# Order of the second-layer sums, of GpSimd's joins and of the splits in a fused attention, expert and softplus kernel

## The chip, the cores and the metric

The kernel runs on one core of one Trainium2 chip. A core has TensorE (matrix products, results in the eight banks of PSUM), VectorE, ScalarE, GpSimd and SyncE, each with an instruction queue of its own that it works through in order; work on different engines is ordered by semaphores. GpSimd does not read PSUM here. The metric is the time of one execution on the device in microseconds, median of the timed runs.

## The reference

Three stages, each feeding the next. Everything is float32, the last stage's weights come as 64-bit floats.

```python
# attention: q, k, v of (4, 8, 576, 64); k and v averaged over groups of 8 positions
attn = softmax(q @ mean8(k).T / sqrt(64));  x = attn @ mean8(v)        # -> (2304, 512)
# 8 experts, all of them for every token, with shares P from 8 rounds of row and column scaling
P = balanced(exp(x @ w_gate))
out = sum(P[:, e:e+1] * (relu(x @ w1[e]) @ w2[e]) for e in range(8))   # 512 -> 1024 -> 512
# softplus stage
return softplus(out @ w_in) @ w_out                                   # 512 -> 2048 -> 512
```

## The kernel before

**Arithmetic.** Every float32 product is made of three products in a shorter format: each operand is split into a rounded part (`hi`, by ScalarE) and the remainder (`lo`, by VectorE or GpSimd), and hi*hi, lo*hi and hi*lo are added in PSUM (`three`, L794). On top of that the large products are done by Winograd's form of Strassen's scheme: a 2 x 2 block product from seven products of sums of blocks.

**Phases and units.** The 2304 tokens are three groups of 768 (`PAIRS`). There are six phases: the expert stage for the three groups (phases 0, 1, 2), then the softplus stage for them (3, 4, 5). A phase of the expert stage has 32 units, one for each 256 columns of the hidden layer (4 to an expert), a softplus phase has 8. A unit `n` has a first part (x times its columns of `w1`) and a second part (the hidden columns times `w2`). The order of the parts is `first 0, first 1, second 0, first 2, second 1, ...` (`todo`).

**Phases 1 and 2** apply the seven-product scheme in both layers, the second over a pair of units, even and odd (`first_twice`, `second_twice`). The first part of a unit is seven products of six matmuls, in the order A11, A22, S2, S1, A12, S3 and, as `rest`, S4. They stand in two double banks of PSUM: `d1` holds `pa` and `pd_`, `d2` holds `pc` and `pb`. A12 goes on top of `pa`, S3 on top of `pb`, S4 on top of `pc`. VectorE adds: `u1 = pb + a` (L865) before S3 is added onto `pb`, then `a = pb + a`, `pb = pc + a`, `pd_ = pd_ + a`, and after S4 `pc + u1`. `a` is a copy of `pa` that ScalarE makes.

**The posts.** The blocks of a finished pair are scaled by the tokens' shares (`shared`, L886) and become seven operands, q to q+6, each with `hi` and `lo`: two from the even unit's blocks and one difference (`even_posts`), the other four with the odd unit's (`odd_posts`). The last step at once is `p3` (L933): two remainders, and then the subtraction of `s3` from `d2` into `s3` (L936). The operands q+4 to q+6 are left in the list `later` as s2, s4, s1 and one more remainder, and `run_later` does them in the first part of the next even unit, right behind u1 (L866). s1 (L943) adds `d2` to `a21`; s4 (L948) subtracts `s3` from `d1`, in its bank.

**Banks.** The first parts of pairs take the double banks of kind R and L in turn (two each), and the form products of the second parts take the other kind: two of them in the even unit's second part (q, q+1), five in the odd unit's (q+2 to q+6), each 12 matmuls. A bank is handed on in the order in which its last reader was issued, so the first of the five form products takes the bank of `d1` or `d2` that was let go first. Behind the first form product of a second part comes S4 of the unit that is under way (`go_on`).

**Beside that**, three kinds of work are handed out by `between(k)`, called after the k-th product of a first part: `to_split` (in the last unit of a phase: the seven splits of the next phase's inputs, a ScalarE cast and a load of the remainder from `xlod` on SyncE's queue), `joins` (GpSimd's sums of blocks for the next phase, in even units; `load_x` and pauses are in this list too), and in odd units `hook` or `convert` (VectorE's conversion of the softplus weights from 64 bits, 32 chunks over the whole kernel, six steps each; those missing when a weight is to be loaded are done at once by `needed`). After the first part come the casts and remainders of the next `w1` (`prep_w1`) and the load of the one after it (`load_w`). In the second parts of phase 0 and of phases 3 to 5 `hook` is called behind each 128 tokens; its argument says whether it may convert.

Of the kernel before, what the change touches and what calls it, by code (L numbers as in the profile page):

```python
# [19 lines left out]
def attention_moe_softplus_kernel(  # L20
# [12 lines left out]
    nc = tc.nc  # L33
# [814 lines left out]
    def first_twice(n, between):  # L848

        product = product_of(n)  # L850
        a, u1 = (zpool.tile([P, TB], F32, tag="z", name=x) for x in ("za", "u1"))
        kind = "RL"[sets[n][3] // 2 % 2]
        d1 = two_banks(kind, "p")
        pa, pd_ = d1[:, 0], d1[:, 1]
        product(pa, A11, "b11")
        between(0)
        product(pd_, A22, "t4")
        nc.scalar.copy(a, pa)
        between(1)
        d2 = two_banks(kind, "p")  # L860
        pc, pb = d2[:, 0], d2[:, 1]
        product(pb, S2, "t2")
        between(2)
        product(pc, S1, "t1")
        vadd(u1, pb, a)  # L865
        run_later()  # L866
        between(3)
        product(pa, A12, "b21", True)
        between(4)
        product(pb, S3, "t3", True)  # L870
        vadd(a, pb, a)
        vadd(pb, pc, a)
        vadd(pd_, pd_, a)
        between(5)
        two_t[n] = d1, d2

        def s4():
            product(pc, S4, "b22", True)
            vadd(pc, pc, u1)

        return s4
# [6 lines left out]
    def form_hi(q, src):  # L888
        nc.scalar.copy(h_slot(q)[0], src)  # L889
# [27 lines left out]
    def odd_posts(n):  # L917

        f, _, _, u = sets[n]
        q = pair_of_units(n) * FORMS  # L920
        d1, d2 = two_t.pop(n)

        def p1():
            shared(d1, d1, 0)
            form_hi(q + 2, d1)

        def p2():
            shared(d2, d2, 1)
            form_hi(q + 3, d2)
            if u % UPE == UPE - 1:  # L930
                load_shares(TWICE.index(f) * E + u // UPE + 1)

        def p3():  # L933
            form_lo(q + 2, d1, nc.vector)
            form_lo(q + 3, d2, nc.vector)
            vsub(s3_t(), d2, s3_t())  # L936

        def s2():
            form_hi(q + 5, s3_t())
            form_lo(q + 5, s3_t(), nc.gpsimd)  # L940

        def s1():
            vadd(a21_t(), d2, a21_t())  # L943
            form_hi(q + 4, a21_t())
            form_lo(q + 4, a21_t(), nc.gpsimd)

        def s4():
            vsub(d1, d1, s3_t())  # L948
            form_hi(q + 6, d1)

        later.extend([s2, s4, s1, lambda: form_lo(q + 6, d1, nc.vector)])
        return [p1, p2, p3]

    def m_at(f, k):
# [601 lines left out]
    for step, (what, n) in enumerate(todo):  # L1556
# [3 lines left out]
        if what == "first":  # L1560
            nxt = sets[n + 1] if n + 1 < len(sets) else None
            if n and sets[n - 1][0] != f:
                xs.update(xs_next)
                xs_next.clear()
            if nxt is not None and n:
                sums_w1(n + 1)
            if nxt is not None and nxt[0] != f:
                flush()
                to_split = splits(x_for(nxt[0]), t_in(t_at[nxt[0]], nxt[2]), f=nxt[0])

            if twice(n):
                if not twice(n - 1):
                    while not between_chunks[0]:
                        convert()
                    settled()
                    open_banks("right", ("R", 2))
                    open_extra(
                        ("hhi", [P, 2 * TB], F32R), ("hlo", [P, 2 * TB], F32R), ("whi", [P, UC * HALF], F32R),
                        ("wlo", [P, UC * HALF], F32R), ("a21", [P, 2, TB], F32), ("s3", [P, 2, TB], F32),
                    )  # L1580

                def between(k):

                    if to_split and k in (1, 3, 4, 5):
                        to_split.pop(0)()
                    if u % 2 == 0:
                        if k == 2:
                            settled()
                        if joins and k in (1, 4):
                            joins.pop(0)()  # L1590
                        return
                    if k == 0:
                        sharing[0] = not side
                        pause[0] = 0
                    if not sharing[0]:
                        hook()
                    elif (k == 0 and u < NU1 - 1) or not between_chunks[0]:
                        convert()

                away[0] = "LR"[u // 2 % 2]  # L1600
                rest = first_twice(n, between)
                prep_w1(n + 1)
                load_w(1, n + 2)
                if pair_of_units(n) == 0 and u % 2:
                    prep_form(2)
                    prep_form(3)
                continue

            if n and twice(n - 1):
                away[0] = "L"  # L1610
                open_banks(*P_BANKS)

            def between(k):

                if to_split and k < 6:
                    to_split.pop(0)()
                if kind == "sp":
                    hook()
                if n or k > 1:
                    hook()  # L1620

            rest = first(n, between, None if n else unit0)
            if not (n and twice(n - 1)):
                pending.pop(0)()
            if [x[0] for x in todo[step + 1:step + 3]] == ["second"] * 2:
                prep_w2(n)
                load_w(2, n + 1)
            if n and not twice(n - 1):
                prep_w1(n + 1)
                load_w(1, n + 2)  # L1630
            if todo[step + 1][0] != "second":
                go_on()
                prep_w2(n)
                load_w(2, n + 1)
                while pending:
                    pending.pop(0)()
        else:
            if twice(n):
                second_twice(n)
                if u == NU1 - 1 and not twice(n + 1):  # L1640
                    assert not joins
                    open_extra(("xl", [P, 2 * TB], F32))
                    open_banks(*Y_BANKS)
                    spare[0] = "c"
                    while pending:
                        pending.pop(0)()
                ahead(f, kind, u)
                continue
            posts = even_posts(n + 1) if twice(n + 1) else []
            behind = n + 1 < len(sets) and todo[step - 1] == ("first", n + 1)  # L1650
            if f == 0 and u == RAW * UPE:
                assert attn[0] is None
                flush()
                shares_to_raw([RAW - 1])
            for i in range(PAIRS[pair] // P):

                second(n, i)
                if i == 0 and posts:
                    posts.pop(0)()
                go_on()  # L1660
                if posts and i:
                    posts.pop(0)()
                if pending:
                    pending.pop(0)()
                if i == 1 and twice(n + 1):
                    prep_form(0)
                    prep_form(1)
                elif i == 1 and behind and n + 1 not in w2_t:
                    prep_w2(n + 1)
                    if kind == "sp" or u % 2:  # L1670
                        load_w(2, n + 2)
                if i == 4:
                    while stores:
                        stores.pop(0)()
                    if behind and kind == "moe" and u % 2 == 0:
                        load_w(2, n + 2)
                if i == 5:
                    while more_stores:
                        more_stores.pop(0)()
                if kind == "moe" or i >= 3:  # L1680
                    hook(i >= 2)
            del h_t[n], w2_t[n]
            while pending:
                pending.pop(0)()
            ahead(f, kind, u)
            if f == 0 and u == NU1 - 6:
                load_shares(0)
            if f == 0 and u == NU1 - 6:
                f64_t.pop()
            if twice(n + 1):  # L1690
                for i in range(2):
                    load_form(2 + i)
                nc.sync.dma_start(gd, g_t[1])
                open_banks("left", ("L", 2))
            if attn[0] is None and "" in banks:
                part_banks()
                tpool = pools[0]
# [30 lines left out]
```

## Time and profile before

| | us |
|---|---|
| median of 3 runs | 1993.35 (1991.28 to 1993.51) |
| the profiled execution's own time | 1996.32 |
| its span | 1994.5 |
| TensorE busy in it | 1955.4 (98%) |
| VectorE / GpSimd / ScalarE busy | 1470.4 / 1476.8 / 977.7 |
| granted clock of TensorE, mean | 0.995 |

The profile is of one execution. Times are from the start of its span. In its rows PE is TensorE, PEld its loading of weights, DVE VectorE, ACT ScalarE, POOL GpSimd, SP SyncE; `q` behind the name means the engine's sequencer, which issues DMAs. A tile is named without its number: `p` is a bank of a first part, `py` of a form product, `u` is u1, `a` is `a21`, `s` is `s3`, `g` one of the large buffers of blocks. The line is that of a helper where one issues the instruction (L845 and L846 are `vadd` and `vsub`, L797 is the matmul of `three`).

### The profile page before, as it was taken

How to read it: one execution, taken by the hardware profiler on the slowest of the kernel's cores; microseconds unless marked ns; L12 is line 12 of the kernel's file. 1: busy time of each engine (PE TensorE's matmuls, PEld its weight loads, DVE VectorE, ACT ScalarE, POOL GpSimd, SP SyncE). 2: the span in 40 equal slices, each digit the busy share in tenths (PEclk: the TensorE clock that was granted, in tenths of full speed). 3: DMA queues.
4: the chain of work that ended last, by engine and by line, in shares of the span. 5: the costliest groups of instructions: out<-in, count | busy, mean ns of one | idle time of the engine just before them, and what ended most of it. 6: DMA issues, size and time to landing. Idle time of an engine off the chain costs nothing.

```text
span 1994.5 us, 30491 instructions
## 1 busy us (share of the span) xinstructions
PE 1955.4 (98%) x10954; PEld 1802.7 (90%) x10954; DVE 1470.4 (74%) x2339; ACT 977.7 (49%) x1777; POOL 1476.8 (74%) x1142
## 2 busy tenths in 40 slices
PE   9899999999999999999999999999999999999999
PEld 7687888888888999999999999999999988888887
DVE  6776576787667788878888778888788776546455
ACT  5545435343334544545445554455454565555542
POOL 5776667777877778777787788887787879666563
PEclk8999999999999999999999999999999999999999
DMA  7443433546547644555455554555545523523411
GB/s 177 129 153 123 142 122 133 175 157 203 178 160 250 197 160 159 168 176 148 158 172 159 199 160 154 164 160 168 179 145 155 179 105 108 201 93 110 140 64 64
DMA packets 213347, 306.56 MB, mean 154 GB/s; under 512 B 33308, under 2 KB 147532, under 8 KB 212940
## 3 DMA queue, kind: packets, MB, share of 16 engines
q1 hardware_dynamic: 203116, 290.85, 45.4%
q10 hardware_dynamic: 10080, 13.77, 1.9%
q8 instruction: 86, 1.41, 0.3%
q14 instruction: 65, 0.53, 0.1%
HBM read 239.30 MB, written 65.27 MB: 153 GB/s over the span
## 4 chain that ended last, share of the span: by engine, by line
PE 79%; POOL 7%; DVE 6%; issue 4%; ACT 2%; DMA 2%; SPq 0%; ACTq 0%; POOLq 0%; DVEq 0%
PE py L797 40%; PE p L797 36%; POOL w1lo L289 3%; POOL w2lo L289 1%; DVE p L846 1%; DVE a L845 1%; PE s L477 1%; PE px L522 1%; POOL g L289 1%; DVE u L845 1%; POOL hlo L893 1%; PE pa L512 1%; ACT w1hi L320 1%; DVE p L1042 0%; DMA qt<-in_q_dram 0%
## 5 line engine op out<-in xcount | busy, mean ns | idle before, releaser
L797 PE MATMUL p<-xhi,w1hi 128*128 128x384 f32 x1680 | 571.9, 340 | 4.8 <-DVE p L1042 2.3
L797 PE MATMUL p<-xlo,w1hi 128*128 128x384 f32 x1680 | 564.1, 336 | 1.6 <-DMA xlo<-xlod 1.6
L797 PE MATMUL p<-xhi,w1lo 128*128 128x384 f32 x1680 | 565.0, 336 | 0.0
L289 POOL TENSOR_TENSOR w2lo<-w2raw,w2hi 128x512 fp32r<-128x512 f32 (+1 forms) x235 | 364.3, 1566 | 124.4 <-ACT w2hi L243 110.7
L289 POOL TENSOR_TENSOR w1lo<-w1raw,w1hi 128x512 fp32r<-128x512 f32 x240 | 239.7, 1022 | 241.2 <-ACT w1hi L320 241.0
L797 PEld LDWEIGHTS p<-xhi,w1hi 128*128 128x128 f32 x1680 | 316.0, 188 | 22.0 <-issue 9.6
L797 PEld LDWEIGHTS p<-xlo,w1hi 128*128 128x128 f32 x1680 | 316.2, 188 | 6.2 <-DMA xlo<-xlod 1.9
L797 PEld LDWEIGHTS p<-xhi,w1lo 128*128 128x128 f32 x1680 | 315.7, 188 | 0.0
L289 POOL TENSOR_TENSOR w1lo<-sums,w1hi 128x1024 fp32r<-128x1024 f32 x120 | 289.5, 2412 | 1.6 <-ACT w1hi L320 1.6
L797 PE MATMUL py<-w2hi,hhi 128*128 128x512 f32 x672 | 270.6, 403 | 4.4 <-DVE g L1129 1.9
L797 PE MATMUL py<-w2lo,hhi 128*128 128x512 f32 x672 | 265.6, 395 | 0.0
L797 PE MATMUL py<-w2hi,hlo 128*128 128x512 f32 x672 | 265.3, 395 | 0.0
L797 PE MATMUL py<-hhi,w2hi 128*128 128x384 f32 x716 | 245.0, 342 | 8.3 <-DVE a L845 8.3
L797 PE MATMUL py<-hhi,w2lo 128*128 128x384 f32 x716 | 241.5, 337 | 3.2 <-POOL w2lo L289 3.1
L845 DVE TENSOR_TENSOR g<-py,g 128x768 f32<-128x768 f32 x210 | 199.7, 951 | 56.7 <-PE py L797 56.7
L797 PE MATMUL py<-hlo,w2hi 128*128 128x384 f32 x716 | 241.0, 337 | 0.0
L889 ACT CAST hhi<-p 128x768 fp32r<-128x768 f32 x128 | 102.7, 802 | 239.9 <-DVE p L886 202.6
L797 PEld LDWEIGHTS py<-w2hi,hhi 128*128 128x128 f32 x672 | 126.2, 188 | 37.7 <-DVE g L1129 4.8
L797 PEld LDWEIGHTS py<-w2hi,hlo 128*128 128x128 f32 x672 | 126.2, 188 | 31.2
L797 PEld LDWEIGHTS py<-hhi,w2hi 128*128 128x128 f32 x716 | 134.5, 188 | 19.5 <-DVE a L845 16.0
L797 PEld LDWEIGHTS py<-w2lo,hhi 128*128 128x128 f32 x672 | 126.3, 188 | 24.1
L797 PEld LDWEIGHTS py<-hhi,w2lo 128*128 128x128 f32 x716 | 134.5, 188 | 5.1 <-POOL w2lo L289 5.1
(164 smaller groups left out, 3561.1 us busy)
## 6 DMA issues: line engine op xcount, KB each, us to landing
w1raw<-in_moe_w_dram SPq DMA_DIRECT2D x96, 512.0 KB
w2raw<-td SPq DMA_DIRECT2D x128, 256.0 KB
sums<-sd SPq DMA_DIRECT2D x62, 512.0 KB
w2raw<-in_moe_w_dram SPq DMA_DIRECT2D x96, 256.0 KB
w2raw<-in_moe_w_dram SPq DMA_DIRECT2D x32, 512.0 KB
sd<-sums SPq DMA_DIRECT2D x32, 512.0 KB
td<-w2raw SPq DMA_DIRECT2D x64, 256.0 KB
xlo<-xlod SPq DMA_DIRECT2D x35, 384.0 KB
```

The source lines that it names most:

```text
L289: nc.gpsimd.tensor_tensor(o, a, b, op=ALU.subtract)
L320: nc.scalar.copy(at(hi), src)
L477: nc.tensor.matmul(ps[:QP, j * 2 * SP:(j + 1) * 2 * SP], qT[:, j * QP:(j + 1) * QP], kb)
L512: nc.tensor.transpose(pa[:SP, j * QP:(j + 1) * QP], ex[:, 2 * j + h, :], ident[:QP, :QP])
L522: nc.tensor.matmul(px[h * D:(h + 1) * D, :W], vp[:, h, :], aT[:, h, :])
L797: nc.tensor.matmul(ps, lhs[a], rhs[b], start=first and i == 0, stop=last and i == 2, skip_group_check=goes_on,)
L845: vadd = lambda o, x, y: nc.vector.tensor_tensor(o, x, y, op=ALU.add)
L846: vsub = lambda o, x, y: nc.vector.tensor_tensor(o, x, y, op=ALU.subtract)
L889: nc.scalar.copy(h_slot(q)[0], src)
L893: eng.tensor_tensor(lo, src, hi.bitcast(F32), op=ALU.subtract)
```

## The change

It has five parts. In `odd_posts`, s1 adds within the bank (`d2`), s4 writes to `a21` in SBUF, the remainder of q+4 is VectorE's and that of q+6 GpSimd's, and the order of the list is s2, s1, s4, remainder. In `first_twice` the first three of the list are issued before the third product, S2, and so before u1 on VectorE; the remainder stays behind u1. In `between` of phases 1 and 2 the splits are handed out one after k = 1, 3 and 4 and three after k = 5, where it was one after each; joins are handed out one in each unit (even: k = 1, odd: k = 2) where it was two in each even unit; the last unit of phase 1 begins a conversion. In the second parts with a `hook`, converting is allowed from the fourth tile on, where it was from the third.

```diff
@@ first_twice
         product(pd_, A22, "t4")
         nc.scalar.copy(a, pa)
         between(1)
+        while len(later) > 1:
+            later.pop(0)()
         d2 = two_banks(kind, "p")
         pc, pb = d2[:, 0], d2[:, 1]
         product(pb, S2, "t2")
@@ odd_posts
         def s1():
-            vadd(a21_t(), d2, a21_t())
-            form_hi(q + 4, a21_t())
-            form_lo(q + 4, a21_t(), nc.gpsimd)
+            vadd(d2, d2, a21_t())
+            form_hi(q + 4, d2)
 
         def s4():
-            vsub(d1, d1, s3_t())
-            form_hi(q + 6, d1)
-
-        later.extend([s2, s4, s1, lambda: form_lo(q + 6, d1, nc.vector)])
+            vsub(a21_t(), d1, s3_t())
+            form_hi(q + 6, a21_t())
+            form_lo(q + 6, a21_t(), nc.gpsimd)
+
+        later.extend([s2, s1, s4, lambda: form_lo(q + 4, d2, nc.vector)])
         return [p1, p2, p3]
@@ between, phases 1 and 2
-                    if to_split and k in (1, 3, 4, 5):
-                        to_split.pop(0)()
+                    for _ in range((0, 1, 0, 1, 1, 3)[k]):
+                        if to_split:
+                            to_split.pop(0)()
                     if u % 2 == 0:
                         if k == 2:
                             settled()
-                        if joins and k in (1, 4):
+                        if joins and k == 1:
                             joins.pop(0)()
                         return
+                    if joins and k == 2:
+                        joins.pop(0)()
                     if k == 0:
                         sharing[0] = not side
                         pause[0] = 0
                     if not sharing[0]:
                         hook()
-                    elif (k == 0 and u < NU1 - 1) or not between_chunks[0]:
+                    elif (k == 0 and (u < NU1 - 1 or twice(n + 1))) or not between_chunks[0]:
                         convert()
@@ second parts with a hook
                 if kind == "moe" or i >= 3:
-                    hook(i >= 2)
+                    hook(i >= 3)
```

## Rows read from the trace of the kernel before

**Rows 1.** Page, first part: busy us (share of the span) xinstructions of each engine.
```profile
PE 1955.4 (98%) x10954; PEld 1802.7 (90%) x10954; DVE 1470.4 (74%) x2339; ACT 977.7 (49%) x1777; POOL 1476.8 (74%) x1142
```

**Rows 2.** Waits of TensorE, 640 to 1600 us: waiter <- releaser: total us, times, longest.
```profile
PE py L797 <- DVE a L845: 10.4, 30, 0.4
PE py L797 <- POOL w2lo L289: 3.1, 5, 0.7
PE p L797 <- DMA xlo<-xlod: 1.6, 1, 1.6
...
PE py L797 <- POOL wlo L289: 0.7, 1, 0.7
```

**Rows 3.** Timeline, TensorE, 902.6 to 904.6 us: start, us, engine, line, operation, tiles [idle before].
```profile
902.65 0.34 PE L797 MATMUL p<-xhi,w1hi 128*128 128x384 f32 x1
...
903.52 0.33 PE L797 MATMUL p<-xhi,w1lo 128*128 128x384 f32 x1
904.21 0.45 PE L797 MATMUL py<-hhi,w2hi 128*128 128x384 f32 x1 [0.36 <-DVE a L845]
904.50 0.34 PE L797 MATMUL py<-hlo,w2hi 128*128 128x384 f32 x1
```

**Rows 4.** Timeline, VectorE, the same pair of units, 900.3 to 906.7 us.
```profile
900.32 0.95 DVE L846 TENSOR_TENSOR s<-p,s 128x768 f32<-128x768 f32 x1
901.87 0.56 DVE L845 TENSOR_TENSOR u<-p,za 128x384 f32<-128x384 f32 x1 [0.60 <-PE p L797]
902.35 0.96 DVE L846 TENSOR_TENSOR p<-p,s 128x768 f32<-128x768 f32 x1
903.21 0.95 DVE L845 TENSOR_TENSOR a<-p,a 128x768 f32<-128x768 f32 x1
...
905.04 0.55 DVE L845 TENSOR_TENSOR za<-p,za 128x384 f32<-128x384 f32 x1
905.63 1.03 DVE L845 TENSOR_TENSOR p<-p,za 128x384 f32<-128x384 f32 x2
```

**Rows 5.** Timeline, VectorE, a pair with a width conversion.
```profile
1021.23 0.95 DVE L846 TENSOR_TENSOR s<-p,s 128x768 f32<-128x768 f32 x1
1022.53 0.56 DVE L845 TENSOR_TENSOR u<-p,za 128x384 f32<-128x384 f32 x1 [0.35 <-PE p L797]
```

**Rows 6.** Timeline, TensorE, the same pair: first matmul of its sixth product.
```profile
1023.31 0.34 PE L797 MATMUL p<-xhi,w1hi 128*128 128x384 f32 x1
```

**Rows 7.** Timeline, VectorE, another pair of units.
```profile
1175.67 0.56 DVE L845 TENSOR_TENSOR u<-p,za 128x384 f32<-128x384 f32 x1 [0.70 <-PE p L797]
```

**Rows 8.** Timeline, TensorE, the same pair: last of the fifth, first of the sixth product.
```profile
1175.92 0.34 PE L797 MATMUL p<-xhi,w1lo 128*128 128x384 f32 x1
1176.28 0.44 PE L797 MATMUL p<-xhi,w1hi 128*128 128x384 f32 x1
```

**Rows 9.** Line L1271, 640 to 1600 us: count: ns min/median/max, first and last start.
```profile
L1271 DVE TENSOR_TENSOR dt<-da,dt x22: 690/691/692, 651.2 to 1563.2; 128x512 f32<-128x512 f32 x22
```

**Rows 10.** Timeline, GpSimd, a pair with joins: the second join, a later remainder.
```profile
1212.07 1.86 POOL L286 TENSOR_TENSOR g<-g,g 128x768 f32<-128x768 f32 x1
...
1218.19 1.31 POOL L289 TENSOR_TENSOR w2lo<-w2raw,w2hi 128x512 fp32r<-128x512 f32 x1
```

**Rows 11.** Timeline, TensorE, the same pair, in its last form product.
```profile
1219.56 0.44 PE L797 MATMUL py<-hhi,w2lo 128*128 128x384 f32 x1 [0.66 <-POOL w2lo L289]
```

**Rows 12.** Timeline, SyncE's queue, end of phase 1: the last three loads of splits.
```profile
1108.05 1.33 SPq L695 DMA_DIRECT2D xlo<-xlod  x3
```

**Rows 13.** Timeline, TensorE, the first unit of phase 2.
```profile
1114.58 0.44 PE L797 MATMUL p<-xlo,w1hi 128*128 128x384 f32 x1 [1.60 <-DMA xlo<-xlod]
```

**Rows 14.** Stretches of one pair each, without and with a conversion: us, then busy us.
```profile
844.42:874.37 29.95, 29.59 (x169) 29.27 (x169) 24.27 (x34) 15.75 (x27) 23.07 (x16) 1.00 0.49 156
1024.87:1055.11 30.24, 29.90 (x169) 29.13 (x169) 26.61 (x37) 14.45 (x24) 23.11 (x17) 1.00 0.49 157
```

**Rows 15.** Timeline, TensorE, second unit of phase 3.
```profile
1640.23 0.44 PE L797 MATMUL p<-xhi,w1hi 128*128 128x384 f32 x1 [0.54 <-DVE p L1042]
```

## The prediction

> **What bounds the kernel now.** I read the page's busy shares first: TensorE is busy for 1955.4 of 1994.5 us [rows 1], so a change of order can gain only idle TensorE time, and can lose without limit. Next the waits of TensorE, cut to the stage that the diff touches, phases 1 and 2 (640 to 1600 us) [rows 2]. One wait repeats: 30 times, about once for each of the 32 pairs of units, a form product waits for VectorE's sum into `a21` (s1, L943). Behind it stand GpSimd's remainders (six times in the list) and one late load of a split. The idle time in that list is less than the loss: around one such wait [rows 3] the matmuls start every 0.17 us (902.65 to 903.52 is five steps), then come 0.69 and 0.29 us, so the loss is 0.52 + 0.12 = 0.64 us where 0.36 us are called idle. I add 0.27 us to each idle of TensorE from here on.
>
> Why the form product waits: VectorE's timeline of the same 4 us [rows 4]. The subtraction of `p3` (L936, `s<-p,s`) starts at 900.32, VectorE then idles 0.60 us until TensorE has finished the unit's fourth product, does u1 (`u<-p,za`, L865), s4 (`p<-p,s`) and s1 (`a<-p,a`), and s1's end at 904.16 lets the form product start at 904.21 [rows 3]: 0.05 us from end to start. s1 is the last reader of the bank that the first form product takes.
>
> I call the start of L936's subtraction v, and the product that adds onto the bank that u1 has read (`S3`, L870) the sixth product. The sixth product may start only when u1 has ended.
>
> **The change, part by part.** Sums before u1: what goes. s4 now leaves `d1` and s1 works inside `d2`; the first form product finds `d1`'s bank free about 1.5 us before it needs it, so the 30 waits go: 30 x 0.63 = -18.9 us.
>
> What comes. On VectorE's queue s1 and s4 now stand between the subtraction and u1; queued behind them are u1, then one remainder, then `za`, and TensorE's sixth product waits for u1. The idle 0.60 us is filled, but two sums are longer than that. How far apart do they start? Two that do not touch each other's data start 0.86 us apart (902.35, 903.21) though each lasts 0.95; one that must wait for the one before starts 0.04 us after its end (`za` at 905.04 lasts 0.55, the next starts at 905.63) [rows 4]. After the change s1 writes `d2`, which the subtraction right before it reads, and s4 writes `a21`, which s1 right before it reads. The trace of before shows no such pair of sums, so I bound it: 0.86 us each if overwriting needs no wait, 0.99 us each if it does. In-order overlap of 0.09 us would let a writer start while the reader still runs, so I take 0.99. Then s1 starts at v + 0.99, s4 at v + 1.98, u1 0.86 later at v + 2.84, ends at v + 3.40, and TensorE starts the sixth product at v + 3.45.
>
> Without a wait it starts at v + 2.33 in a pair without a width conversion (902.65 against 900.32 [rows 3, 4]) and at v + 2.08 in one with (1023.31 against 1021.23 [rows 5, 6]); there the conversion has made VectorE later. The new wait is 1.12 and 1.37 us, with 0.12 us to get going again 1.24 and 1.49 us. u1's slack now is only 0.22 us (902.65 less its end, 902.43). That this product does wait for u1 is seen once already: in the pair at 1175 us u1 starts late at 1175.67 and ends at 1176.23 [rows 7], and the sixth product starts at 1176.28, 0.36 us behind the matmul before it instead of 0.17 [rows 8].
>
> How many: of the 30 pairs two, the first of each phase, have the subtraction far enough ahead and get no new wait; 22 conversions end in this stage [rows 9], two of them in those first pairs. That leaves 20 pairs with a conversion and 8 without: 20 x 1.49 + 8 x 1.24 = +39.7 us. With 0.86 us each the sum would be 28 x 0.26 = 7.3 us less: +32.4.
>
> The Trainium skill has a rule on this: VectorE: DVE Perf Modes, "The DRAIN you can't avoid", says that the next Vector instruction starts when the pipe is empty and that a semaphore between two costs nothing extra. By it a waiting sum would cost no more than another. The rows above differ: 0.86 us apart without a wait, and a start after the end with one, so the rows decide here and the rule is kept as rival 2.
>
> The rest of that move is covered. The remainder of q+4 goes from GpSimd to VectorE and that of q+6 the other way: the same instruction counts. VectorE's `hlo<-p,hhi` now runs while TensorE does the sixth product. GpSimd's second remainder waits for s4's form instead of s1's and is needed two form products (4.1 us) later. ScalarE's three casts come up to 1 us sooner, ahead of the `w1` casts. No cost.
>
> Joins one to a unit. In the pairs where GpSimd joins, two additions of about 1.86 us stand in the even unit's queue ahead of the remainder that the last form product needs; that ends at 1219.50 and TensorE idles 0.66 us [rows 10, 11]. One of the two now goes into the odd unit, behind the last remainder of the pair, so the needed one comes 1.8 us sooner, and TensorE itself is later by the new wait: these waits go whole. Six in the list: 3.1 + 0.7 + 6 x 0.27 = -5.4 us. Cover: GpSimd's idle time in the odd unit; if it were gone, the 5.4 us stay.
>
> Splits ahead of a load. At the end of phase 1 the last three `xlo` loads are issued on SyncE's queue at 1108.05 [rows 12], behind those for `w1raw` and `sums`, and TensorE idles 1.60 us for one of them at 1114.58 [rows 13]: 1.87 us. Two of the three now go one form product and one product (3.1 us) sooner and ahead of these loads, which are passed by them and come some 2 us later, needed only a unit on: -1.9 us. ScalarE's casts of these splits pass the `w1` casts, which have 5 us until their product. But this pair then has the ordinary new wait, +1.5. Net -0.4. At the end of phase 2 the wait is another one (banks reopened), and stays.
>
> Conversions. The last odd unit of phase 1 now converts one more chunk: a pair with one takes 30.24 us against 29.95 [rows 14], +0.3. In exchange one chunk fewer should be forced at the start of phase 3, where a forced one costs 0.54 + 0.27 = 0.8 us [rows 15]. Phase 0 gives up the conversion step behind its third token tile, which may leave one chunk more for phase 3 or spare a collision in phase 0. I bound both together by that row, from -1.6 to +0.8, and take -0.8.
>
> **Sum.** -18.9 + 39.7 - 5.4 - 0.4 + 0.3 - 0.8 = +14.5 us. The profiled execution took 1996.3 us itself and would take 2010.8; it lies 3 us over the median of the three timed runs, 1993.35, against which I forecast 2007.8.
>
> **The rivals.** (1) Faster. The bank is freed and nothing is late in its place: u1 does not set the sixth product's start. Then 18.9 + 5.4 + 1.9 go and the conversions change nothing that counts: 1993.35 - 26.2 = 1967.2. It decides where u1 ends before TensorE gets there, that is if the sums took under 0.4 us each or the subtraction came 1.1 us sooner. For it: the wait for a bank is the one that repeats. Against it: u1's slack of 0.22 us, and VectorE's unbroken queue before v. The Trainium skill (Perfetto Trace Analysis, "Optimization Strategy") says that a gap that repeats on the busiest engine can mean too little PSUM for the next tile; the trace agrees on the cause of the 0.36 us idle, but not on what a freed bank would bring. (2) Overwriting costs no wait, sums 0.86 us apart: 7.3 us less, 2000.5. For it: nothing is read back. Against: order on one engine is kept by waits where data is read back. (3) The first form product still takes the bank of `d2`, now freed last, so the change doesn't do what it says. The remainder that frees it ends near v + 4.3, the sixth product near v + 4.6: no further cost, the same time. (4) GpSimd's joins still hold up the last form product: 5.4 us more, 2013.2. (5) The new wait is half of what I think, since posts on VectorE come sooner than in the trace of before: about 20 us less, 1988 to 1997.
>
> **How the numbers follow.** My forecast, 2003 to 2011: 0.53. Rival 2, 1998 to 2003: 0.20. Rival 4: 0.05. Rival 1: 0.11. Rival 5: 0.11, of it 0.08 within 0.2% (1989.4 to 1997.3; about what a measurement of this kernel can tell from no change) and 0.03 faster. Rival 3 shares the forecast's time. Range 1997 to 2012: it leaves out rivals 1, 4 and 5. Faster 0.14, same 0.08, slower 0.78.
>
> **What would show it.** In the waits of TensorE, `py <- DVE a` gone; in its place `p <- DVE u L845` some 28 times, 0.85 to 1.25 us idle each. Pairs without a conversion 30.5 us long instead of 29.9, with one 31.1 instead of 30.2; pairs with joins no longer than those. VectorE: no idle time between the subtraction and u1, and 0.99 us from start to start of the two sums (0.86: rival 2). No wait for `w2lo` in the last form product, none for `xlo` near 1114 us. Pairs of 29.3 us would make me wrong outright: u1 would then not be what the sixth product waits for.

## The result and the profile after

The changed kernel takes 2010.75 us (median of 4 runs, 2006.96 to 2014.06), the kernel before 1992.63 us beside it: a ratio of 1.0091 [1.0072, 1.011], 18 us slower. The profiled execution took 2006.96 us itself, its span 2005.1 us.

The waits of TensorE, 640 to 1600 us of the changed kernel (waiter <- releaser: total us, times, longest):

```profile
PE p L797 <- DVE u L845: 29.9, 29, 1.1
PE py L797 <- ACT whi L243: 0.3, 1, 0.3
```

Against [rows 2], the form product's 30 waits for `a` are gone, GpSimd's and the load's too, and 29 waits of the sixth product for u1 stand in their place. How one arises, in the pair that answers to [rows 3, 4]: the timeline of VectorE, then the first matmul of the sixth product (start, us, engine, line, operation, tiles [idle before]).

```profile
901.22 0.94 DVE L846 TENSOR_TENSOR s<-p,s 128x768 f32<-128x768 f32 x1
902.08 0.96 DVE L845 TENSOR_TENSOR p<-p,a 128x768 f32<-128x768 f32 x1
903.08 0.96 DVE L846 TENSOR_TENSOR a<-p,s 128x768 f32<-128x768 f32 x1
903.95 0.55 DVE L845 TENSOR_TENSOR u<-p,za 128x384 f32<-128x384 f32 x1
```

```profile
904.55 0.44 PE L797 MATMUL p<-xhi,w1hi 128*128 128x384 f32 x1 [0.84 <-DVE u L845]
904.83 0.34 PE L797 MATMUL p<-xlo,w1hi 128*128 128x384 f32 x1
```

From the subtraction (v = 901.22) VectorE goes without idle time through s1, s4 and u1. u1 ends at 904.50 and TensorE starts at 904.55, 0.84 us idle. In the list of pairs the idle time is 1.09 to 1.12 us in the 21 pairs with a conversion and 0.84 to 0.88 us in the 8 without.

The same in stretches of one pair each (us, then busy us of TensorE, its weight loads, VectorE, ScalarE, GpSimd, granted clock, DMA share, GB/s; behind each x the number of instructions): without a conversion, with one, and with one and GpSimd's joins.

```profile
844.84:875.30 30.46, 29.62 (x170) 29.30 (x169) 24.17 (x33) 15.72 (x27) 23.07 (x17) 1.00 0.51 158
1028.24:1059.19 30.95, 29.85 (x169) 29.09 (x169) 26.60 (x37) 14.44 (x25) 23.07 (x17) 1.00 0.51 154
1213.64:1244.67 31.03, 29.93 (x169) 29.20 (x169) 26.59 (x37) 14.46 (x25) 26.52 (x19) 1.00 0.49 157
```

The first two answer to [rows 14]: +0.51 and +0.71 us a pair.

But the pairs are not the whole. Each unit's first part has one copy on ScalarE (`za<-p`), and its times cut the span into parts that can be compared. Here units 16 and 31, both in phase 0, in the kernel before:

```profile
372.54 0.48 ACT L1046 COPY za<-p 128x384 f32<-128x384 f32 x1 [1.58 <-PE p L797]
612.18 0.48 ACT L1046 COPY za<-p 128x384 f32<-128x384 f32 x1 [0.38 <-PE p L797]
```

and in the changed one:

```profile
368.02 0.48 ACT L1048 COPY za<-p 128x384 f32<-128x384 f32 x1 [0.45 <-PE p L797]
610.98 0.48 ACT L1048 COPY za<-p 128x384 f32<-128x384 f32 x1 [6.10 <-PE p L797]
```

Unit 16 stands 4.52 us earlier. This is the start of the span, not the change: in the first 50 us the granted clock was 0.86 in the execution shown of before and 1.00 in that of after, and the kernels below that have phase 0 as before stand 0.5 to 4.9 us earlier at unit 16. From unit 16 to unit 31 it took 239.64 us before and 242.96 after: phase 0 is 3.3 us longer.

All kernels of this study, by the same copies (unit 16 to 31; 33 to 96, which is phases 1 and 2; 96 to 99, the start of phase 3; differences to the kernel before, in us, from the profiled executions) and by their medians. The ratios are to the kernel before run beside each: its median there was 1992.63 us for the changed kernel, 1994.2 for e1, e2, e3 and v1, 1995.32 for e4 to e7, 1993.15 for e8 and e9. So medians of different groups compare to some 3 us only.

| kernel | phase 0 | phases 1, 2 | start of phase 3 | median us | ratio to before |
|---|---|---|---|---|---|
| before | 239.64 | 954.70 | 50.95 | 1992.63 | |
| changed | +3.32 | +12.2 | 0.0 | 2010.75 | 1.0091 [1.0072, 1.011] |
| e1, sums alone | 0.0 | +13.4 | 0.0 | 2008.5 | 1.007 [1.0055, 1.0085] |
| e2, all but the sums | +8.19 | -5.2 | 0.0 | 1995.1 | 1.0004 [0.9994, 1.0014] |
| e3, changed, step back | 0.0 | +11.4 | -1.6 | 2001.99 | 1.0038 [1.0025, 1.005] |
| e6, changed, early store | +0.1 | +11.2 | 0.0 | 2003.21 | 1.0039 [1.0026, 1.0052] |
| e8, e2 with step back | 0.0 | -5.9 | -1.6 | 1983.75 | 0.9954 [0.9936, 0.9972] |
| e9, phase 0's step alone | +4.6 | +1.4 | 0.0 | 2001.79 | 1.0035 [1.0024, 1.0046] |
| e4, e3 with no sum ahead | 0.0 | -1.6 | -1.6 | 1987.2 | 0.9957 [0.9942, 0.9972] |
| e5, e3 with one sum ahead | 0.0 | -16.3 | -1.6 | 1974.97 | 0.9899 [0.9885, 0.9912] |
| e7, both ahead, old places | 0.0 | +8.9 | -1.3 | 1998.98 | 1.0021 [1.0009, 1.0033] |
| v1, new order | 0.0 | -18.9 | -1.3 | 1972.18 | 0.9886 [0.9872, 0.9899] |

"Step" is the conversion step behind phase 0's third token tile, which the change gives up.

### The profile page after: what moved, and what is told of

The parts are those of the page before. It is cut to its first block, busy times and chain, and to the rows that moved or that the text cites. A ratio compares the mean times of both kernels' runs of the same rounds, so it can differ in the third digit from the quotient of the medians.

```text
span 2005.1 us, 30540 instructions
## 1 busy us (share of the span) xinstructions
PE 1948.3 (97%) x10954; PEld 1798.4 (90%) x10954; DVE 1469.3 (73%) x2339; ACT 977.1 (49%) x1777; POOL 1477.1 (74%) x1142
## 4 chain that ended last, share of the span: by engine, by line
PE 76%; DVE 17%; ACT 2%; issue 2%; DMA 1%; POOL 1%; SPq 0%; ACTq 0%; DVEq 0%; POOLq 0%
PE py L797 39%; PE p L797 34%; DVE p L845 3%; DVE g L845 2%; DVE hlo L895 2%; DVE p L888 2%; DVE s L846 1%; DVE dt L1273 1%; DVE u L845 1%; DVE dt L1272 1%; PE s L477 1%; PE px L522 1%; DVE za L845 1%; PE pa L512 1%; POOL w1lo L289 1%
## 5 line engine op out<-in xcount | busy, mean ns | idle before, releaser
L895 POOL TENSOR_TENSOR hlo<-s,hhi 128x768 fp32r<-128x768 f32 x64 | 118.7, 1855 | 48.9 <-ACT hhi L891 42.2
```

The source lines that it names most:

```text
L895: eng.tensor_tensor(lo, src, hi.bitcast(F32), op=ALU.subtract)
```

## The experiments

The theory: u1, queued on VectorE behind two sums, makes the sixth product late, and that is the loss. The rivals: the other edits make it, or the new places of the sums (bank and SBUF) do. A second question came up with the traces: why phase 0 is longer.

### The sums alone, and everything but the sums

e1 is the kernel before with these two edits:

```diff
         between(1)
+        while len(later) > 1:
+            later.pop(0)()
         d2 = two_banks(kind, "p")
@@ odd_posts
-            vadd(a21_t(), d2, a21_t())      # s1
+            vadd(d2, d2, a21_t())
-            vsub(d1, d1, s3_t())            # s4
+            vsub(a21_t(), d1, s3_t())
-        later.extend([s2, s4, s1, lambda: form_lo(q + 6, d1, nc.vector)])
+        later.extend([s2, s1, s4, lambda: form_lo(q + 4, d2, nc.vector)])
```

The casts and remainders of q+4 and q+6 move with their sums as in the change; they are left out here.

> The kernel before with only the sums' part of the change: s1 inside d2's bank, s4 into a21, both and s2 issued ahead of the third product's addition u1; joins, splits, conversions and phase 0 as before. My theory: the loss is u1 standing behind these two sums on VectorE, so this kernel alone has it whole: 30 waits of 0.63 us gone (-18.9), 21 new ones of 1.37 us in pairs with a conversion and 8 of 1.11 us in pairs without (+37.7), together +18.8 us, about 2011 us. The rival, that joins, splits, conversions or phase 0 made the loss: the 30 waits go and little comes, about 1974 us.

Measured: 2008.5 us, +14. The waits of TensorE, 640 to 1600 us:

```profile
PE p L797 <- DVE u L845: 28.6, 28, 1.1
PE p L797 <- DMA xlo<-xlod: 0.9, 1, 0.9
PE py L797 <- POOL w2lo L289: 0.6, 2, 0.3
```

The sums alone make most of the loss, 14 of 18 us. It is some 5 us less than I had expected, and 4 of these are seen: GpSimd's waits [rows 2] fell from 3.8 to 0.6 us and the load's from 1.6 to 0.9 us without any edit to them. A TensorE that is late elsewhere waits less for them.

e2 is the opposite: the changed kernel with `first_twice` and `odd_posts` as before.

> The changed kernel with the sums put back as they were before; joins one to a unit, splits ahead of a load, the conversion step of phase 1's last odd unit and the one that phase 0 gives up stay. My theory: GpSimd's joins -5.4 us, the late split -1.9, a conversion +0.3, and phase 0 +3.3 if the step that it gives up is the cause of the longer phase 0 seen in the changed kernel (about 1989 us), 0 if that was chance (about 1985.6). The rival, that this rest is what made the kernel slower: 1993 us or more, with the 30 waits of 0.36 us still there.

Measured: 1995.1 us, no gain. In phases 1 and 2 the trace has 5.2 of the 7.0 us expected there (5.4 + 1.9 - 0.3), but phase 0 took 8.2 us more. That sets two tasks: undo the step in phase 0, and find why it costs.

### Phase 0's step

```diff
-                    hook(i >= 3)
+                    hook(i >= 2)
```

e3 is the changed kernel with this:

> The changed kernel with phase 0's conversion step behind the third token tile put back, all else as changed. If giving up that step is what made phase 0 3.3 us longer, this one is 3.3 us faster than the changed kernel (about 2007.4 us) and its last unit of phase 0 stands as early against unit 24 as in the kernel before. If the longer phase 0 was chance, the time stays at about 2010.7 us.

Measured: 2001.99 us, 8.8 us less than the changed kernel, where one trace had shown, and the expectation had taken, 3.3. Phase 0 is as long as before, and the start of phase 3 is 1.6 us shorter. There the waits of TensorE, 1610 to 2000 us, in the changed kernel, then in e3:

```profile
PE p L797 <- DVE p L1044: 1.1, 2, 0.5
PE py L797 <- DVE g L1116: 0.5, 1, 0.5
```

```profile
PE p L797 <- DVE p L1044: 0.5, 1, 0.5
```

One forced chunk fewer, and with it two waits of 0.5 us, one in a first part and one in a second part: with 0.27 us added to each, 1.6 us. In the changed kernel the extra conversion of phase 1's last unit had only replaced the one that phase 0 gave up.

e8 makes the same edit to e2, e9 gives the step up in the kernel before and changes nothing else:

> The kernel before with joins one to a unit, splits ahead of a load and the conversion step of phase 1's last odd unit; sums and phase 0 as before. It tells why these parts, run together with phase 0's given-up step, brought nothing (1995.1). My theory: they are worth what the trace of that run shows in phases 1 and 2, 5.2 us, and one forced chunk less in phase 3, 1.6 us, and the given-up step took it back: about 1987 to 1988 us, with phase 0 as long as in the kernel before. The rival, that these parts bring nothing by themselves: about 1994 us.

> The kernel before with phase 0's conversion step behind the third token tile given up, and nothing else. My theory: the finished chunk that is not stored holds a tile, the splits' remainders wait for their stores, and phase 0 is 3 to 8 us longer (3.3 and 8.1 in the two traces that have it); one more chunk is forced in phase 3, 1.6 us: about 1999 to 2004 us. The rival, that the longer phase 0 needs the other edits too: 1994 to 1996 us.

Measured: 1983.75 and 2001.79 us. The first is 3 to 4 us less than expected, the second as the theory has it but for the place of e9's extra forced chunk: it begins at 1656.95 us, behind the copy of unit 99, and from that copy on the span is 2.7 us longer. So this step alone costs 0.35% [0.24, 0.46], some 7 us (in the trace 2.7 of them are the forced chunk), and it had eaten the gain of e2.

Where it costs, in the changed kernel: TensorE, then VectorE.

```profile
572.76 0.40 PE L797 MATMUL py<-w2hi,hlo 128*128 128x512 f32 x1
575.03 0.51 PE L797 MATMUL py<-w2hi,hhi 128*128 128x512 f32 x1 [1.87 <-DVE xl L741]
```

```profile
571.35 0.55 DVE L811 SCALAR_TENSOR_TENSOR hlo<-p,hhi 128x384 fp32r<-128x384 f32 x1
574.42 0.56 DVE L741 TENSOR_TENSOR xl<-g,xh 128x384 fp32r<-128x384 f32 x1 [2.52 <-DMA xlod<-xl]
574.89 0.75 DVE L1131 SCALAR_TENSOR_TENSOR g<-py,prob,g 128x512 f32<-128x512 f32 x1
```

A split's remainder `xl` waits 2.52 us on VectorE for the store of the one before, and the sum behind it (`g<-py`) hands TensorE its bank late: 2.15 of the 3.3 us of phase 0. The rest is a smaller wait of TensorE at 539 us. In e2 the same wait lasted 5.07 us. The code says which resource it is: `xl` and the conversion's result `dt` take turns in two tiles (tag "ex"). With the step given up, phase 0's sixth chunk (the expectation of e6 calls it the seventh) is finished at 467 us but is stored only at 577 us (`v<-dt`), since no later step comes to issue the store. Until then it holds one of the two tiles, so all fourteen remainders of phase 0 go through the other, where they alternate in the kernel before.

e6 issues this store in unit 24 and leaves everything else as changed (the second edit holds back the load that would go with an early store, since in the changed kernel none goes with it):

```diff
                     hook(i >= 3)
+                    if i == 2 and f == 0 and u == 24:
+                        early[0] = True
+                        settled()
@@ from_float64, done
-                fetch(at)
+                if not (early[0] and at == 1):
+                    fetch(at)
```

> The changed kernel, in which the store of phase 0's seventh finished chunk is issued in unit 24 instead of unit 30, and no more: the conversion step stays given up. My theory of the longer phase 0: this finished but unstored chunk holds one of the two tiles that the splits' remainders (xl) take in turn, so each remainder waits for the store of the one before, up to 5 us, on VectorE ahead of the sum that frees TensorE's bank. With the store early the remainders alternate again, VectorE's waits for the stores near 575 us go, and the time falls from 2010.75 by 3 to 7 us, to about 2004 to 2007 us (not to the 2002.0 of the kernel with the step back, since one more chunk is forced in phase 3, 1.6 us). The rival, that the missing step itself shifts the work against the loads: 2010.7 us, with the wait for xl still there.

Measured: 2003.21 us, 7.5 us less than the changed kernel and just under the expected 2004, with the step still given up. Phase 0 is at +0.1 us, and the remainder follows at once:

```profile
572.07 0.55 DVE L811 SCALAR_TENSOR_TENSOR hlo<-p,hhi 128x384 fp32r<-128x384 f32 x1
572.53 0.54 DVE L741 TENSOR_TENSOR xl<-g,xh 128x384 fp32r<-128x384 f32 x1
573.00 0.74 DVE L1131 SCALAR_TENSOR_TENSOR g<-py,prob,g 128x512 f32<-128x512 f32 x1
```

So the held tile is the cause, not the missing step.

### Order against places, and how many sums

The next four have phase 0's step back, so they stand against e3. e4 takes the loop in front of `d2` out again (both sums behind u1, new places). e5 keeps only s1 ahead of u1:

```diff
-        while len(later) > 1:
+        while len(later) > 2:
             later.pop(0)()
```

e7 has the loop, but s1 into `a21` and s4 inside `d1` as before.

> The changed kernel with both sums behind u1 again but in their new places (s1 inside d2's bank, s4 into a21), and phase 0's conversion step back. The form product then takes d1's bank, which s4 frees as the last of u1, s1, s4. My theory: u1 is not late, so no wait of the sixth product; the form product waits again, and for s4 0.14 us longer than it did for s1 in the kernel before, since s4 overwrites a21, which s1 reads, and starts 1.00 us after it instead of 0.86: 30 x (0.51 + 0.14) = +19.5 us over the version with the new order (1972.2), about 1992 us. The rival, that the new places by themselves free the bank in time: about 1972 us.

> The changed kernel with one sum ahead of u1, s1, and s4 behind it; new places; phase 0's conversion step back. My theory, that only the length of the queue ahead of u1 counts: u1 starts at v + 0.86 + 0.87 = v + 1.73 and ends at v + 2.28; the sixth product would start at v + 2.33 in a pair without a conversion (no wait) and at v + 2.08 in one with (0.25 us late): 21 x 0.25 = +5.3 us over the version with the new order (1972.2), about 1977.5 us, and no wait for a bank. The rival, that each sum ahead of u1 costs its whole step: 29 x 0.87 = +25 us, about 1997 us.

> The places of the kernel before (s1 into a21, s4 inside d1's bank) with both sums ahead of u1; joins, splits and conversions as changed, phase 0's step back. It parts the order from the places. My theory: the order alone makes the loss, and only the 0.14 us that s4 waits to overwrite a21 is due to the places: the kernel with the step back (2002.0) less 29 x 0.14 = 4 us, about 1998 us, with 29 waits for u1 of about 0.95 us. The rival, that the new places made it: no wait for u1, about 1972 us. If overwriting costs nothing at all: 2002 us.

Measured: none ahead 1987.2 us, one 1974.97 us, two 2001.99 us (e3), two in the old places 1998.98 us. The waits of TensorE, 640 to 1600 us, of e4, then of e7:

```profile
PE py L797 <- DVE a L846: 15.2, 31, 0.5
```

```profile
PE p L797 <- DVE u L845: 26.0, 29, 1.0
```

With no sum ahead the old wait for the bank is back, now for s4 and 0.5 us instead of 0.4; with both ahead it is the wait for u1 whatever the places. e4 against e8, the same but for the places and the order of the two sums, has phases 1 and 2 longer by 4.3 us in the trace (3.5 us by medians, 0.6 by ratios): the new places free no bank in time. With one sum ahead the wait is just what the sum says. VectorE and TensorE of e5, a pair with a conversion:

```profile
1044.27 0.95 DVE L846 TENSOR_TENSOR s<-p,s 128x768 f32<-128x768 f32 x1
1045.14 0.96 DVE L845 TENSOR_TENSOR p<-p,a 128x768 f32<-128x768 f32 x1
1046.00 0.55 DVE L845 TENSOR_TENSOR u<-p,za 128x384 f32<-128x384 f32 x1
```

```profile
1046.17 0.34 PE L797 MATMUL p<-xhi,w1lo 128*128 128x384 f32 x1
1046.60 0.44 PE L797 MATMUL p<-xhi,w1hi 128*128 128x384 f32 x1
```

u1 ends at v + 2.28, and the sixth product starts 0.43 us behind the matmul before it instead of 0.17: 0.26 us late, in 21 pairs. In the others it starts on time, and only its second matmul is 0.1 us late. By the time, e4 and e5 are 5 and 2.5 us under what was expected of them; both were reckoned from v1, which has a small wait of its own (see below) that they lack.

The spacing of the sums settles the open price. In e7, where no sum overwrites what the one before reads:

```profile
897.24 0.95 DVE L846 TENSOR_TENSOR s<-p,s 128x768 f32<-128x768 f32 x1
898.11 0.95 DVE L845 TENSOR_TENSOR a<-p,a 128x768 f32<-128x768 f32 x1
898.97 0.96 DVE L846 TENSOR_TENSOR p<-p,s 128x768 f32<-128x768 f32 x1
899.84 0.55 DVE L845 TENSOR_TENSOR u<-p,za 128x384 f32<-128x384 f32 x1
```

All three steps are 0.86 or 0.87 us, and the idle time before the sixth product falls from 0.84 to 0.71 us and from 1.09 to 0.96 us.

### A version made from this

v1 keeps joins, splits and the extra conversion, leaves phase 0 alone, and puts the sum that frees the needed bank first behind u1:

```diff
         vadd(u1, pb, a)
-        run_later()
+        while len(later) > 1:
+            later.pop(0)()
@@
         vadd(pd_, pd_, a)
+        run_later()
@@ odd_posts, s1 into a21 and s4 in d1 as before the change
-        later.extend([s2, s4, s1, lambda: form_lo(q + 6, d1, nc.vector)])
+        later.extend([s2, s1, s4, lambda: form_lo(q + 6, d1, nc.vector)])
```

> A version made from the theory: u1 first, as before, then s1 (into a21, so it frees d2's bank one sum sooner), then s4 inside d1's bank, then the three additions of the running unit, and the last remainder behind them; joins, splits and conversions as in the changed kernel, phase 0 as before. My theory: the form product gets its bank 0.86 us sooner and needs it 0.52 us sooner, so its 30 waits go; u1 is where it was, so the sixth product does not wait: -18.9 - 5.4 - 1.9 + 0.3 = -25.9 us, about 1967 us. The rival, that a freed bank only moves the wait: the second form product would wait for the last remainder, or the seventh product for the additions, some 0.5 us in each of 30 pairs, about 1982 us.

Measured: 1972.18 us, 0.9886 [0.9872, 0.9899], faster than both kernels. VectorE, then TensorE around the end of the sixth product:

```profile
1041.71 0.56 DVE L845 TENSOR_TENSOR u<-p,za 128x384 f32<-128x384 f32 x1 [0.35 <-PE p L797]
1042.19 0.95 DVE L845 TENSOR_TENSOR a<-p,a 128x768 f32<-128x768 f32 x1
```

```profile
1043.38 0.34 PE L797 MATMUL p<-xhi,w1lo 128*128 128x384 f32 x1
1043.56 0.33 PE L797 MATMUL py<-hhi,w2hi 128*128 128x384 f32 x1
```

s1 ends at 1043.14 and the form product follows without a gap. Of the expected 25.9 us, 22 came by the medians, and 18.9 in phases 1 and 2 of the trace. Two pieces of the rest are visible. At the end of phase 1 there is a new wait for ScalarE's `whi`, 1.4 us idle; what makes it was not shown. And in 29 pairs the last of the five form products starts late, by too little to stand in the list of waits. VectorE, then TensorE:

```profile
844.31 0.95 DVE L845 TENSOR_TENSOR g<-py,g 128x768 f32<-128x768 f32 x1
```

```profile
845.17 0.34 PE L797 MATMUL py<-hhi,w2lo 128*128 128x384 f32 x1
845.41 0.41 PE L797 MATMUL py<-hhi,w2hi 128*128 128x384 f32 x1
845.66 0.34 PE L797 MATMUL py<-hlo,w2hi 128*128 128x384 f32 x1
```

The two steps are 0.24 and 0.25 us instead of 0.17: 0.14 us a pair, 4.2 us in all. In each of these pairs the product starts 0.15 us after the end of VectorE's `g<-py`, which by its place reads the bank of the form product two before; so it very likely waits for that bank. In e8 and e5 this is seen once. The rival of v1 was thus right in part: some of the wait has moved, 0.14 us a pair where it said 0.5.

## Why the prediction was right, and where it was off

The forecast was 2007.8 us (1997 to 2012), the median is 2010.75 us; against the kernel before it was +14.5 us, and +18.1 us was measured. By its own steps:

- The mechanism: as forecast. `py <- DVE a` is gone, u1 is late behind s1 and s4, the sixth product waits 29 times (28 forecast, and one more in the term of the splits), and the gain of the freed bank is more than spent. e1 shows that these edits alone make 14 of the 18 us, e4, e5 and e3 that it goes by the number of sums ahead of u1, e7 that the places hardly matter.
- The size of the new wait: 1.37 and 1.11 us of loss a pair, each with 0.27 us added to the idle time, where I had 1.49 and 1.24. The step that failed is "0.99 us each". Only s4 waits to overwrite: it starts 1.00 us behind s1, but s1 starts 0.86 us behind the subtraction though it overwrites `d2`, which the subtraction reads. u1 comes at v + 2.73, not v + 2.84. Over 29 waits that is 3.6 us. Rival 2, by which neither waits, is half right. The rule of the Trainium skill that went with it (VectorE: DVE Perf Modes, "The DRAIN you can't avoid": a semaphore between two costs nothing extra) does not hold here for s4: 1.00 us in the new places, 0.86 us in the old.
- Joins: the waits for `w2lo` are gone as forecast, and the pair with joins (31.03 us) is hardly longer than one without (30.95). With the splits the part is worth 5.9 us beside the old sums (e8), where 5.4 + 1.9 - 0.3 = 7.0 follow from my terms, but only 2 us of the trace beside the new ones (e3 against e1; 6.5 us by the medians, 1.6 of them at the start of phase 3), which take most of these waits away by themselves. I had priced the two parts as if they added up.
- The late load is gone as forecast. "No cost" for ScalarE's casts is in doubt: there is a new wait for `whi`, 0.3 us here and 1.4 us in v1, but none in e3 and e6, and what makes it was not shown.
- Phases 1 and 2 together: +15.3 forecast, +12.2 in the trace. The difference is the 3.6 us above, less the wait for `whi`.
- Conversions and phase 0: this step failed. I had bounded it from -1.6 to +0.8 us by the price of a forced chunk and taken -0.8. It is +3.3 us in the trace and more in the runs: 7.0 us by e9, 7.5 us by the medians of e6 and of the changed kernel, 10 us by their ratios. The bound came from a row of phase 3, and I did not ask what else the step does: it issues the store that gives a tile back, and the splits need that tile. e3 shows that with the tile given back the start of phase 3 has the gain I had named, at 1.6 us twice its size, since a forced chunk brings two waits and I had priced one.
- The other rivals: 1 is out by the time, 4 by the waits for `w2lo` that are gone, 5 by the length of the new waits. Which bank the first form product took (rival 3) was not looked at; by its own words it would not show in the time.
- So the total came out close in part by luck, because two errors had opposite signs: 3 us too much for phases 1 and 2, and 4 us (by the trace) to 8 or 11 us (by the runs) too little for phase 0.

Open is why the wait for the store differs so much between executions (2.5, 3.2 and 5.1 us in three traces). In the changed kernel the store went out at 567.12 us and was waited for until 574.4 us; from 570.5 to 575 us the DMA engines were 94% busy, in e9 from 569.9 to 574.1 us 100%. That loads and the store compete there is likely, but nothing was run to show it.

## What to carry to other kernels

Before moving work ahead of an instruction on an in-order queue, add up start to start what then stands between the last event that holds and that instruction, and compare it with the slack of the one who waits for it: here 0.22 us of slack took one sum for 0.26 us and two for 1.1 to 1.4 us. When a bank is released late, try first the order of its readers behind the critical instruction: v1 against e8 is 11.6 us faster (13.0 in phases 1 and 2 of the traces). They differ in that order and in the place of the last remainder, which v1 puts behind the running unit's additions. The waits that went were for s1, which stands ahead of that remainder in both; the remainder's move alone was not run. When a step is taken out, list everything that it issues, the stores and the tiles that they give back among it, and who shares these tiles.

## What was unexpected in the hardware

Two dependent sums on VectorE, the second overwriting what the first reads, started 0.86 us apart in one case (`s<-p,s`, then `p<-p,a`, the bank read and overwritten in place) and 1.00 us apart in the other (`p<-p,a`, then `a<-p,s`), each 0.95 us long. In the trace only the second pair has a wait between the two: `p<-p,a` waits for no semaphore, `a<-p,s` for one that VectorE itself raises.

After an idle time of 1.87 us TensorE's granted clock stayed at 1.00. After 2.56 us (e9) and 4.43 us (e2) it was 0.54 and 0.50, the lower of its two levels (1.2 GHz), in the next 3.5 us, so the long wait in phase 0 costs more than its idle time. These are three single executions. The stretch in e2 behind the wait, and its matmuls, 0.43 us apart instead of 0.23:

```profile
577.80:581.50 3.70, 3.70 (x9) 2.93 (x10) 2.46 (x4) 0.00 (x0) 2.85 (x4) 0.50 0.67 251
```

```profile
577.78 0.80 PE L797 MATMUL py<-w2hi,hhi 128*128 128x512 f32 x1 [4.43 <-DVE xl L741]
578.38 0.63 PE L797 MATMUL py<-w2lo,hhi 128*128 128x512 f32 x1
578.80 0.63 PE L797 MATMUL py<-w2hi,hlo 128*128 128x512 f32 x1
```

That makes up most of the 8.2 us of e2's phase 0: 4.6 us for the wait, 12 matmuls at half speed for some 2.5 us, and 1 us in a smaller wait at 539 us.
